# Linformer attention with a squared-ReLU feed-forward: both first products of batch 0 ahead of its second ones, woven streams from batch 1's first chunk on, one pool of nine slots for h and x sums

## The chip, the cores and the metric

One core of a Trainium2 chip runs the whole kernel. The time is that of the device, in microseconds (us), as the median of several executions. Differences under 0.3% (1.4 us) are about what a measurement of this kernel can't tell from no change.

In the lines of the profile PE is TensorE (matmuls), PEld its weight loads, DVE is VectorE, ACT is ScalarE, POOL is GpSimd (here it only issues loads), SP is SyncE (here it only issues stores and DMA transposes). A "q" behind the name (SPq, ACTq) is that engine's sequencer. L652 is line 652 of the kernel before.

## What is computed

There are 8 batches with 8 heads, 1024 tokens and a head size of 64; everything arrives in float32.

```python
k_proj = np.einsum('ks,bhsd->bhkd', E, k)        # E, F: 64 x 1024
v_proj = np.einsum('ks,bhsd->bhkd', F, v)
attn = softmax(q @ k_proj^T / sqrt(64))          # over the 64 projected keys
x = (attn @ v_proj) as 8192 tokens x 512
out = np.maximum(x @ w_in, 0)**2 @ w_out         # w_in 512 x 2048, w_out 2048 x 512
```

Here `softmax` and the line of `x` stand for the reference's own few lines. By far the most work is in the two products of the last line.

## The kernel before

**Chunks and stages.** A batch `b` has two chunks `(b, 0)` and `(b, 1)` of 512 tokens. For each chunk attention makes the rows `xT` (channels on the partitions), the first product makes `h = relu(x w_in)^2`, and the second product makes 512 x 512 outputs. Class `Attention` has the attention of a batch, class `Chunk` the two products of a chunk, class `Group` a quarter of a chunk's first product.

**Two forms of a product.** The plain form (`first_mm` L489, `second_mm` L495) has 64 matmuls of 512 columns for each product of a chunk. The seven-product form splits the matrices into halves and takes 7 products of half size instead of 8 (Strassen's scheme in Winograd's form): 112 matmuls of 256 columns (`Group.product` L652, `half_product` L549, `quantum` L572). It needs sums of the operands, which DVE makes: `sum_w_in` and `sum_w_out` once for the weights, `sum_x` for a chunk's `x`, `sum_h` for its `h`, all in `tt` (L150). Its partial results are kept by ACT and added by DVE.

**Order.** The order on PE is written out by hand; every other engine's order is made by the framework from that program, and each engine works off its own instructions in order. Parts of the program are generators that yield after each step, and `at(step, ...)` puts other work (attention, sums, loads) behind that step. The order before is:

1. Head: the projections `E`, `F`, the attention of chunk (0, 0), and warming matmuls.
2. `first_cold` for (0, 0): its first product in plain form. Then `second_cold`: its second product, also plain, because the sums of `w_out` don't exist yet. The attention of chunk (0, 1) is put between.
3. `first_plain` for (0, 1), with `sum_h`, then `second_seven` for (0, 1). The attention of batch 1 for both chunks at once lies beside it.
4. `first_plain` for (1, 0), with a part of the attention of batch 2.
5. From then on two streams are woven: `firsts` (the first products in seven-product form from chunk (1, 1) on, 28 steps a chunk) and `seconds` (`second_spread`, the second products from chunk (1, 0) on, one step behind). A step is four matmuls of each stream. One batch is 56 steps; the attention of batch b + 2 or b + 1 and the loads of batch b + 3 are placed by step numbers.
6. `second_seven` for the last chunk, by itself.

**Attention in the woven stage.** Counted from the first step of a chunk (b, 0), the projection of batch b + 1 (`project`, L258 and L259) lies behind step 2 and its scores for the first pair of heads (`scores`, L329) behind step 16. Between them: DVE copies the projected keys out of PSUM (`kp`, four copies, L246 and L247), SP issues a DMA transpose of 128 KB that makes `kT` out of `kp` (`transpose_k_dma`, L295), and PE's scores wait for that `kT`. The loads of the K and V of the batch after it (1 MB each once in SBUF, issued by POOL at L89 into the only buffers `K_sb` and `V_sb`) wait only until the projection has read the old ones, so they are issued right behind it. `transpose_q_dma` (L321) makes `qT` in the same way, much earlier.

**PSUM and buffers.** Four banks (`bank0` to `bank3`) are handed out in turn by `bank()`. Pairs of banks for attention (`att_psum`): two in the stages 1 to 3, one later, when the other pair is lent to the second products. The tiles of `h` have 7 slots, those of `x_sum` 2 in another pool; a slot is taken in turn, so a new tile waits until the readers of the tile that held the slot are done.

**Loads.** POOL issues all loads in program order, at most eight under way. Half of batch 0's Q (token halves 4 to 7 of each group of 8) is loaded behind the weights, just ahead of the last quarter of `w_out`.

Of the kernel before, what the change touches and what calls it, by code (L numbers as in the profile page):

```python
# [9 lines left out]
P = 128  # L10
F32 = mybir.dt.float32
BF16 = mybir.dt.bfloat16
# [7 lines left out]
def kernel(  # L20
# [11 lines left out]
    nc = tc.nc  # L32

    B, H, S, D = q.shape
# [5 lines left out]
    NI = 8  # L40
    NPAIR = H // 2
    NCB = C // P
# [3 lines left out]
    HC = TCH // 2  # L46
    WP = 4
# [6 lines left out]
    HF, HM = NFB // 2, DM // 2  # L54
# [9 lines left out]
    part_pool = ctx.enter_context(tc.tile_pool(name="part", bufs=5))  # L64
    out_pool = ctx.enter_context(tc.tile_pool(name="outp", bufs=3))
    psum = ctx.enter_context(tc.tile_pool(name="ps", bufs=1, space=bass.MemoryType.PSUM))
    turn = {"att": 0, "bank": 0, "pairs": 2}

    lent = ctx.enter_context(ExitStack())
    pair_pools = [psum, lent.enter_context(tc.tile_pool(name="ps_lent", bufs=1, space=bass.MemoryType.PSUM))]  # L70
# [7 lines left out]

    def bank(shape=(P, 512), dtype=F32, n=None):
        if n is None:  # L80
            turn["bank"] += 1
            n = turn["bank"]
        return psum.tile(list(shape), dtype, tag=f"bank{n % 4}", name="ps_bank")

    def tokens(src, b, h=slice(None), i=slice(None)):
        return src[b].rearrange("h (p i) d -> p h i d", i=NI)[:, h, i, :]

    def load(t, src):
        return nc.gpsimd.dma_start(t, src)  # L89
# [15 lines left out]
    half = (slice(0, 4), slice(4, 8))  # L105
# [21 lines left out]
    for j, (lo, hi) in enumerate(W_IN_PIECES):  # L127
        t = wpool.tile([P, NCB, (hi - lo) * P], BF16, name=f"w_in_{lo}")
        load(t[:], w_in_view[:, :, lo * P:hi * P])
        for fb in range(lo, hi):  # L130
            w_in_at[fb] = (t, fb - lo)
        if j < 2:
            load(V0[:, V_PIECES[j + 1]], tokens(v, 0, h=V_PIECES[j + 1]))
    fn = NFB // WP
    for j in range(WP):
        if j == WP - 1:
            load(Q0[:, :, 4:8, :], tokens(q, 0, i=slice(4, 8)))
        t = wpool.tile([P, fn, DM], BF16, name=f"w_out_{j}")
        load(t[:], w_out_view[:, j * fn:(j + 1) * fn, :])
        w_out_sb.append(t)  # L140
# [31 lines left out]
                    *(w_out_sum[:, n, f] for n in range(4)),  # L172
                )

    def sum_w_in(behind):
        with tc.issue_after(behind.queued.ins):
            for lo, hi in W_IN_PIECES[:3]:
                up, (t, j) = w_in_at[lo][0], w_in_at[HF + lo]
                down = t[:, :, j * P:(j + hi - lo) * P]
                n = NCB // 2  # L180
                left_sums(
                    up[:, 0:n], up[:, n:NCB], down[:, 0:n], down[:, n:NCB],
                    *(w_in_sum[:, m, :, lo:hi].rearrange("p c f k -> p c (f k)") for m in range(4)),
                )
# [37 lines left out]
    class Attention:  # L222
# [16 lines left out]
        def load_q(self):  # L239
            self.Q = load_batch("Q_sb", q, self.b)  # L240


        def keep_k(self, ps_k, g, second=None):
            view = ps_k.rearrange("k (h d) -> k h d", d=D)
# [52 lines left out]
            )  # L297


        def transpose_q_chunk(self, c, src, hg):  # L300
            ps = bank([P, 4, 2, P], BF16)
            for hh in range(4):
                for n in range(2):
                    nc.tensor.transpose(
                        ps[:, hh, n, :],
                        src[:, 4 * hg + hh, 4 * c + 2 * n:4 * c + 2 * n + 2, :].rearrange("p i d -> p (i d)"), ident[:]
                    )
            nc.vector.tensor_copy(self.qT[:, 4 * hg:4 * hg + 4, 2 * c:2 * c + 2, :], ps[:])

        def transpose_q(self, pr):  # L310
            ps = bank([P, 2, NT, P], BF16)
# [126 lines left out]
    class Chunk:  # L438
# [5 lines left out]

        def h_tile(self, kh, part):
            if (kh, part) not in self.h:
                self.h[kh, part] = form_pool.tile([P, 2, HF // 2, HC], BF16, name="h", tag="h", bufs=7)
            return self.h[kh, part]

        def sum_x(self):  # L450
            self.x_sum = x_pool.tile([P, 4, NCB // 2, HC], BF16, name="x_sum")
            n = NCB // 2
            x = [self.xT[:, m:m + n, self.c, a] for m in (0, n) for a in range(2)]
            right_sums(*x, *(self.x_sum[:, m] for m in range(4)))
# [253 lines left out]
    with tc.manual_schedule(engines={PE}):  # L708
# [30 lines left out]
        def at(step, fn, *args, **kwargs):  # L739
            plan.setdefault(step, []).append(lambda: fn(*args, **kwargs))  # L740
# [7 lines left out]
        def run_all(*parts):  # L748
            step = 0
            for part in parts:  # L750
                step = run(part, step)
            assert not plan, plan
# [13 lines left out]
        at(2, att.project_v, V_PIECES[2])  # L766
        at(3, att.chunk_values, 0, 1, (1,))
        at(3, nxt.load_kv)
        at(18, sum_w_in, chunk[0, 0])
        at(21, att.transpose_q_chunk, 1, Q0, 0)  # L770
        at(21, att.transpose_q_chunk, 1, Q0, 1)
        at(21, nxt.load_q)
        at(23, att.chunk_scores, 1, 0)
        at(23, att.chunk_scores, 1, 1)
        at(25, att.sums, 0)
        at(27, att.chunk_values, 1, 0)
        at(27, att.chunk_values, 1, 1)
        at(28, sum_w_out, att)
        at(28, begin, 2)
        at(36, nxt.project)  # L780
        at(36, lambda: atts[2].load_kv())
        at(39, nxt.transpose_q, 0)
        at(39, nxt.transpose_q, 1)
        at(39, nxt.transpose_k)
        at(41, nxt.scores, 0)
        at(41, nxt.scores, 1)
        at(44, nxt.transpose_q, 2)
        at(44, nxt.transpose_q, 3)
        at(44, lambda: atts[2].load_q())
        at(45, nxt.sums, 0)  # L790
        at(47, nxt.scores, 2)
        at(49, nxt.scores, 3)
        at(50, nxt.values, 0)
        at(52, nxt.values, 1)
        at(53, nxt.sums, 2)
        at(59, nxt.values, 2)
        at(60, nxt.values, 3)
        at(60, chunk[1, 1].sum_x)
        at(61, lambda: atts[2].project())
        at(59, begin, 3)  # L800
        at(60, lambda: atts[3].load_kv())
        at(61, lambda: atts[2].transpose_q_dma())
        at(61, lambda: atts[3].load_q())
        run_all(chunk[0, 0].first_cold(), chunk[0, 0].second_cold(), chunk[0, 1].first_plain(), chunk[0, 1].second_seven(*(bank()[:] for _ in range(3))))

        nxt = atts[2]
        at(1, nxt.transpose_k)
        at(3, nxt.scores, 0)
        at(5, nxt.scores, 1)
        at(7, nxt.sums_spread, 0)  # L810
        at(9, nxt.scores, 2)
        at(11, nxt.scores, 3)
        turn["pairs"] = 1
        run_all(chunk[1, 0].first_plain())
        lent.close()
        second_pool = ctx.enter_context(tc.tile_pool(name="ps_second", bufs=1, space=bass.MemoryType.PSUM))

# [7 lines left out]
        def firsts():  # L825
            old = None
            for b in range(1, B):
                for c in range(2):
                    if (b, c) == (1, 0):
                        continue  # L830
                    for g in range(4):
                        new = Group(chunk[b, c], g)
                        for f in F_STEPS:
                            if f is not Group.p4:
                                f(new)
                            elif old:
                                f(old)
                            yield
                        old = new
            for f in F_STEPS:  # L840
                if f is Group.p4:
                    f(old)
                yield

        def seconds():
            for _ in range(LAG):
                yield
            for b in range(1, B):
                for c in range(2):
                    if (b, c) == (B - 1, 1):  # L850
                        return
                    yield from chunk[b, c].second_spread(second_bank)
# [7 lines left out]
        def on(step, b, name, *args):  # L860
            at(step, lambda: getattr(atts[b], name)(*args))

        for b in range(1, B - 1):
            t = 56 * (b - 1)
            if b > 1:
                on(t + 1, b + 1, "scores", 3)
            on(t + 3, b + 1, "sums_spread", 2)
            on(t + 7, b + 1, "values", 0)
            on(t + 10, b + 1, "values", 1)
            on(t + 20, b + 1, "values", 2)  # L870
            on(t + 23, b + 1, "values", 3)
            for c in range(2):
                at(t + 24 + 9 * c, lambda b=b, c=c: chunk[b + 1, c].sum_x())
            if b + 2 < B:
                on(t + 2, b + 2, "transpose_q_dma")
                if b + 3 < B:
                    at(t + 2, begin, b + 3)
                    on(t + 3, b + 3, "load_q")
                on(t + 30, b + 2, "project")
                on(t + 32, b + 2, "transpose_k_dma")  # L880
                if b + 3 < B:
                    on(t + 34, b + 3, "load_kv")
                on(t + 44, b + 2, "scores", 0)
                on(t + 47, b + 2, "scores", 1)
                on(t + 50, b + 2, "sums_spread", 0)
                on(t + 53, b + 2, "scores", 2)
        steps = both()
        run(steps)
        assert not plan, plan
# [31 lines left out]
```

The softmax here doesn't subtract the row's maximum and nothing guards it: scores larger than these inputs give would overflow.

## Time and profile before

| what | value |
|---|---|
| median of 7 executions | 480.8 us (480.54 to 483.25) |
| profiled execution, its own time | 482.66 us |
| its span on the core | 480.8 us |
| granted TensorE clock, mean | 1.00 |
| busy: PE, PEld, DVE, ACT, POOL | 98%, 73%, 73%, 60%, 7% |
| first plain product of (0, 0), PE | 20.69 to 37.68 us |
| second plain product of (0, 0), with the attention of (0, 1) | 37.68 to 54.51 us |
| first product of (0, 1) begins, second begins | 54.51, 75.13 us |
| first product of (1, 0) begins | 93.19 us |
| woven streams begin | 109.99 us |
| last lone second product ends | about 477 us |

How to read it: the span is the time from the first to the last instruction on the core; the 1.9 us between the span and the profiled execution's own time lie around it. "Busy" on PE counts modelled ends of pipelined matmuls, so 98% says that PE nearly always has something under way, not that it is at its peak. In a timeline each line is: start, length, engine, line, operation, tiles, shape, how many instructions were merged, and in brackets the idle time before it with what ended it. A DMA line under SP or POOL is the time of issuing; when the data have landed is told in another view, as microseconds from issue to landing.

### The profile page before, as it was taken

The page shows a single profiled execution, that of the slowest core. Times are in us where ns is not written, and L with a number is a line of the kernel's source. Part 1 is how long each engine was busy: PE and PEld are TensorE (multiplying, and loading weights), DVE is VectorE, ACT ScalarE, POOL GpSimd, SP SyncE. Part 2 cuts the span into 40 slices and gives each one's busy share as a digit, 9 for nine tenths or more (in the row PEclk, how much of TensorE's full clock was granted, in tenths as well). Part 3 has the DMA queues.
Part 4 walks back from the last instruction along what each step waited for, and adds up shares of the span by engine and source line. Part 5 has one row for each costly group of instructions (what it writes and reads, how often), then busy time and mean ns, then how long its engine had stood idle before and what let it go on. Part 6 is the DMA issues. An engine that isn't in the chain of part 4 may idle for free.

```text
span 480.8 us, 10012 instructions
## 1 busy us (share of the span) xinstructions
PE 469.3 (98%) x4096; PEld 352.1 (73%) x4106; DVE 350.0 (73%) x613; ACT 286.7 (60%) x466; POOL 32.6 (7%) x45
## 2 busy tenths in 40 slices
PE   8999999999999999999999999999999999999996
PEld 3444445637878788787878878787887778888885
DVE  2356898856996679767897579966797688967671
ACT  2564567397557774678546784477745775565641
POOL 7410020200010000100000000100000000000000
PEclk9999999999999999999999999999999999999999
DMA  9999998999949497767949499495811054101012
GB/s 179 204 206 205 225 150 149 169 228 193 195 85 181 111 204 170 117 136 183 192 110 177 96 220 177 88 166 136 201 60 55 23 132 111 67 23 67 24 65 89
DMA packets 80046, 66.98 MB, mean 139 GB/s; under 512 B 30720, under 2 KB 76032, under 8 KB 80000
## 3 DMA queue, kind: packets, MB, share of 16 engines
q0 software_dynamic: 30640, 29.23, 39.2%
q1 hardware_dynamic: 49216, 36.97, 29.0%
q8 instruction: 32, 0.52, 0.4%
q10 hardware_dynamic: 144, 0.13, 0.1%
q14 instruction: 14, 0.11, 0.1%
HBM read 59.24 MB, written 16.78 MB: 158 GB/s over the span
## 4 chain that ended last, share of the span: by engine, by line
PE 86%; DVE 8%; ACT 4%; issue 1%; DMA 1%; DVEq 0%; ACTq 0%
PE ps_bank L652 34%; PE ps_second L572 33%; PE ps_bank L489 6%; PE ps_att L329 2%; PE ps_att L258 2%; PE ps_second L549 2%; PE ps_att L405 2%; DVE rs L373 1%; DVE w_in_sum L150 1%; DVE w_out_sum L150 1%; PE ps_bank L216 1%; DVE xT L434 1%; DVE h L150 1%; DMA e_f<-in_E_dram 1%; ACT h L485 1%
## 5 line engine op out<-in xcount | busy, mean ns | idle before, releaser
L150 DVE TENSOR_TENSOR h<-h 128x1024 bf16<-128x1024 bf16 (+1 forms) x182 | 107.9, 616 | 39.8 <-ACT h L662 26.0
L652 PE MATMUL ps_bank<-x_sum,w_in_sum 128*128 128x256 bf16 x624 | 93.9, 273 | 0.0
L652 PEld LDWEIGHTS <-w_in_sum 128*128 128x128 bf16 x832 | 78.7, 98 | 16.2 <-issue 7.5
L572 PEld LDWEIGHTS <-h 128*128 128x128 bf16 x832 | 81.3, 98 | 11.8 <-issue 2.2
L544 ACT COPY u<-ps_bank 128x512 f32<-128x512 f32 x107 | 63.2, 591 | 26.0 <-PE ps_bank L652 23.1
L662 ACT ACTIVATE h<-ps_bank 128x512 bf16<-128x512 f32 x104 | 63.0, 605 | 26.3 <-PE ps_bank L652 25.9
L666 DVE CUSTOM_DVE_ANT_0 h<-ps_bank,u 128x512 bf16<-128x512 f32 x104 | 68.9, 685 | 12.5 <-PE ps_bank L652 11.9
L677 ACT COPY ps_bank<-ps_bank 128x512 f32<-128x512 f32 x52 | 29.7, 570 | 68.9 <-PE ps_bank L652 68.9
L652 PEld LDWEIGHTS <-w_in 128*128 128x128 bf16 x624 | 58.8, 98 | 13.9 <-issue 7.2
L572 PEld LDWEIGHTS <-s 128*128 128x128 bf16 x624 | 61.1, 98 | 7.1
L652 PE MATMUL ps_bank<-xT,w_in 128*128 128x256 bf16 x416 | 62.5, 273 | 0.0
L572 PE MATMUL ps_second<-w_out_sum,s 128*128 128x256 bf16 x416 | 62.4, 273 | 0.0
L572 PE MATMUL ps_second<-w_out_sum,h 128*128 128x256 bf16 x416 | 62.2, 273 | 0.0
L572 PE MATMUL ps_second<-w_out,h 128*128 128x256 bf16 x416 | 60.1, 272 | 1.3 <-ACT ps_second L588 1.3
L409 DVE TENSOR_TENSOR xT<-ps_att,rs 128x512 bf16<-128x512 f32 x56 | 36.0, 684 | 15.9 <-PE ps_att L405 15.9
L489 PE MATMUL ps_bank<-xT,w_in 128*128 128x512 bf16 x186 | 44.6, 379 | 2.1 <-DVE xT L434 1.0
L485 ACT ACTIVATE h<-ps_bank 128x512 bf16<-128x512 f32 x48 | 28.1, 606 | 16.1 <-PE ps_bank L489 15.9
L150 DVE TENSOR_TENSOR o_sb<-ps_second,u 128x512 f32<-128x512 f32 x27 | 18.5, 684 | 25.9 <-PE ps_second L572 20.7
L489 PEld LDWEIGHTS <-w_in 128*128 128x128 bf16 x192 | 17.7, 98 | 24.6 <-issue 6.2
L343 ACT ACTIVATE expT<-ps_att 128x1024 bf16<-128x1024 f32 x32 | 32.9, 1036 | 3.0 <-PE ps_att L329 2.5
L652 PE MATMUL ps_bank<-x_sum,w_in 128*128 128x256 bf16 x208 | 31.4, 273 | 0.0
L652 PE MATMUL ps_bank<-xT,w_in_sum 128*128 128x256 bf16 x208 | 31.3, 273 | 0.0
(104 smaller groups left out, 477.5 us busy)
## 6 DMA issues: line engine op xcount, KB each, us to landing
out_dram<-o_sb SPq DMA_DIRECT2D x63, 256.0 KB, 2.4
rs<-inv SPq DMA_DIRECT2D x96, 128.0 KB, 3.1
K_sb<-in_k_dram POOLq DMA_DIRECT2D x7, 1024.0 KB, 9.7
V_sb<-in_v_dram POOLq DMA_DIRECT2D x7, 1024.0 KB, 15.7
Q_sb<-in_q_dram POOLq DMA_DIRECT2D x7, 1024.0 KB, 12.2
w_out<-in_moe_w_out_dram POOLq DMA_DIRECT2D x4, 512.0 KB, 18.1
w_in<-in_moe_w_in_dram POOLq DMA_DIRECT2D x3, 512.0 KB, 14.9
k_f<-in_k_dram SPq DMA_DIRECT2D x1, 512.0 KB, 4.6
```

The costliest lines, as they stand in the source:

```text
L150: return nc.vector.tensor_tensor(out=o, in0=x, in1=y, op=op)
L258: nc.tensor.matmul(ps[LO, :], lhsT=ET[:, i, :], rhs=self.K[:, :, i, :], start=f, stop=l)
L343: nc.scalar.activation(e[:], ps[:], AF.Exp, scale=SCALE)
L409: nc.vector.tensor_tensor(out=self.xT[:, pr, :, par], in0=ps_x[par].rearrange("p (c t) -> p c t", c=2), in1=rs[:, par].rearrange("p (c t) ...
L485: nc.scalar.activation(h, ps.rearrange("p (a t) -> p a t", a=2), AF.Relu)
L489: nc.tensor.matmul(ps[:], lhsT=w_in_blk(cb, fb), rhs=self.xT[:, cb, self.c].rearrange("p a t -> p (a t)"), start=(cb == 0), stop=(cb == NC ...
L544: nc.scalar.copy(u[:], ps)
L572: nc.tensor.matmul(ps[:, i * HM:(i + 1) * HM], lhsT=self.h_form(n, fb)[:, i * P:(i + 1) * P], rhs=w_out_form(n, fb), start=fresh and i == ...
L652: nc.tensor.matmul(ps[:, j * HC:(j + 1) * HC], lhsT=w_in_form(n, cb, 2 * self.g + j), rhs=self.chunk.x_form(n, cb), start=fresh and j == 0 ...
L662: nc.scalar.activation(self.out(kh, a), ps[:], AF.Relu)
L666: nc.vector._custom_dve(TENSOR_ADD_SAT, out=self.out(kh, a), in0=ps[:], in1=more[:], s0=3.0e38, s1=0.0)
L677: nc.scalar.copy(self.chain[:], self.first[:])
```

## The change

Chunk (0, 0)'s second product no longer follows its first one. Both first products of batch 0 run first, (0, 0) then (0, 1), both plain. Then (0, 0)'s second product runs in the seven-product form. The woven streams begin with the first product of (1, 0) beside the second product of (0, 1), so that `firsts` covers one chunk more and `seconds` one more.

So that this can be: batch 0's late half of Q is loaded earlier, in two pieces; the attention of (0, 1) lies inside the first product of (0, 0) and takes the form by chunk (`chunk_scores`, `chunk_sums`, `chunk_values`); so does batch 1's, of which Q is loaded in two halves and whose first four transposes are copied by ACT; the weight sums are made within the first products, `sum_h` of both chunks of batch 0 is placed by hand; `h` and `x_sum` share nine slots, taken in turn. In the woven stage of each later batch the projection moves from behind step 2 of a chunk (b, 0) to behind step 5 (t + 30 becomes t + 33 with the same origin for the other numbers), its DMA transpose from t + 32 to t + 34 and the loads behind it from t + 34 to t + 36, while the scores stay behind step 16 (t + 44); `sum_x` of the batch's second chunk moves from t + 33 to t + 51. The first pass (b = 0) has its own numbers.

```diff
-    turn = {"att": 0, "bank": 0, "pairs": 2}
+    turn = {"att": 0, "bank": 0, "step": 1, "pairs": 2}
...
             load(V0[:, V_PIECES[j + 1]], tokens(v, 0, h=V_PIECES[j + 1]))
+        if j == 2:
+            for g in range(2):
+                load(Q0[:, half[g], 4:8, :], tokens(q, 0, h=half[g], i=slice(4, 8)))
     for j in range(WP):
-        if j == WP - 1:
-            load(Q0[:, :, 4:8, :], tokens(q, 0, i=slice(4, 8)))
...
-    def sum_w_in(behind):
+    def sum_w_in(behind, piece):
         with tc.issue_after(behind.queued.ins):
-            for lo, hi in W_IN_PIECES[:3]:
+            for lo, hi in W_IN_PIECES[piece:piece + 1]:
...
+        def load_q_halves(self):
+            self.Q = qkv_pool.tile([P, H, NI, D], BF16, name="Q_sb")
+            for i in (slice(0, 4), slice(4, 8)):
+                load(self.Q[:, :, i, :], tokens(q, self.b, i=i))
...
-                self.h[kh, part] = form_pool.tile([P, 2, HF // 2, HC], BF16, name="h", tag="h", bufs=7)
+                self.h[kh, part] = form_pool.tile([P, 2, HF // 2, HC], BF16, name="h", tag="h", bufs=9)
...
-            self.x_sum = x_pool.tile([P, 4, NCB // 2, HC], BF16, name="x_sum")
+            self.x_sum = form_pool.tile([P, 4, NCB // 2, HC], BF16, name="x_sum", tag="h", bufs=9)
...
+        at(6, att.transpose_q_chunk, 1, Q0, 0)
+        at(7, att.transpose_q_chunk, 1, Q0, 1)
+        at(7, nxt.load_q_halves)
+        at(7, att.chunk_scores, 1, 0)
+        at(8, att.chunk_scores, 1, 1)
+        at(9, att.chunk_sums, 1, 0)
+        at(10, att.chunk_sums, 1, 1)
+        at(12, att.chunk_values, 1, 0)
+        at(14, att.chunk_values, 1, 1)
+        for n, step in enumerate((9, 17, 18)):
+            at(step, sum_w_in, chunk[0, int(n > 0)], n)
+        at(18, chunk[0, 0].sum_h, 0)
+        at(20, chunk[0, 0].sum_h, 1)
+        at(22, sum_w_out, chunk[0, 1])
+        at(31, nxt.transpose_q_chunk, 0, None, 0, nc.scalar.copy)
+        at(24, begin, 2)
+        run_all(chunk[0, 0].first_cold(), chunk[0, 1].first_plain(sums=False))
...
+        at(1, nxt.transpose_q_chunk, 0, None, 1, nc.scalar.copy)
+        at(2, nxt.project)
+        at(5, nxt.transpose_k)
+        at(7, nxt.chunk_scores, 0, 0)
+        at(8, nxt.chunk_scores, 0, 1)
+        at(8, nxt.transpose_q_chunk, 1, None, 0)
+        at(9, nxt.chunk_sums, 0, 0)
+        at(10, nxt.chunk_sums, 0, 1)
+        at(10, nxt.transpose_q_chunk, 1, None, 1)
+        at(11, nxt.chunk_values, 0, 0)
+        at(12, nxt.chunk_values, 0, 1)
+        at(12, chunk[1, 0].sum_x)
+        at(12, chunk[0, 1].sum_h, 0)
+        at(12, nxt.chunk_scores, 1, 0)
+        at(14, nxt.chunk_sums, 1, 0)
+        at(14, chunk[0, 1].sum_h, 1)
+        run_all(chunk[0, 0].second_seven(*banks))
...
+        on(1, 1, "chunk_scores", 1, 1)
+        on(5, 1, "chunk_values", 1, 0)
+        on(11, 1, "chunk_sums", 1, 1)
+        on(14, 1, "chunk_values", 1, 1)
+        for b in range(B - 1):
+            t = 56 * (b - 1) + 28
...
-            for c in range(2):
-                at(t + 24 + 9 * c, lambda b=b, c=c: chunk[b + 1, c].sum_x())
+                at(t + 24, lambda b=b: chunk[b + 1, 0].sum_x())
+            at(t + 51, lambda b=b: chunk[b + 1, 1].sum_x())
...
-                on(t + 30, b + 2, "project")
-                on(t + 32, b + 2, "transpose_k_dma")
+                on(t + (33 if b else 35), b + 2, "project")
+                on(t + (34 if b else 36), b + 2, "transpose_k_dma")
                 if b + 3 < B:
-                    on(t + 34, b + 3, "load_kv")
-                on(t + 44, b + 2, "scores", 0)
+                    on(t + (36 if b else 38), b + 3, "load_kv")
+                on(t + (44 if b else 45), b + 2, "scores", 0)
```

## The prediction

> **What bounds the kernel now.** I read the page first: the share of each engine and the chain that ended last.
>
> ```profile
> PE 469.3 (98%) x4096; PEld 352.1 (73%) x4106; DVE 350.0 (73%) x613; ACT 286.7 (60%) x466; POOL 32.6 (7%) x45
> ...
> PE 86%; DVE 8%; ACT 4%; issue 1%; DMA 1%; DVEq 0%; ACTq 0%
> ```
>
> TensorE sets the end, so the time is PE's work plus the holes in it. Next I asked for the stretch from 30 to 140 us: PE is busy 107.65 of 110 us. So the early stages hold few holes, and the woven stage nearly none. Then the timeline of PE gave the prices.
>
> ```profile
> 105.66 4.49 PE L489 MATMUL ps_bank<-xT,w_in 128*128 128x512 bf16 x20
> 109.99 0.60 PE L652 MATMUL ps_bank<-xT,w_in 128*128 128x256 bf16 x4
> ...
> 139.52 0.61 PE L652 MATMUL ps_bank<-x_sum,w_in 128*128 128x256 bf16 x4
> ...
> 142.59 0.60 PE L652 MATMUL ps_bank<-x_sum,w_in_sum 128*128 128x256 bf16 x4
> 143.44 1.03 PE L572 MATMUL ps_second<-w_out,h 128*128 128x256 bf16 x8 [0.26 <-ACT ps_second L588]
> ...
> 151.74 0.60 PE L572 MATMUL ps_second<-w_out_sum,s 128*128 128x256 bf16 x4
> 152.27 0.41 PE L329 MATMUL ps_att<-qT,kT 64*64 64x512 bf16 x4
> 152.61 0.61 PE L652 MATMUL ps_bank<-x_sum,w_in 128*128 128x256 bf16 x4
> ```
>
> Starts, not lengths, are the prices. 20 wide matmuls start from 105.66 to 109.99: 0.2165 us each. A group of four narrow ones takes 0.437 us, a woven step of two groups 0.874. The scores start 0.53 after the group before them and hold PE 0.34: a visit of small attention products costs 0.44 in all. Eight transposes cost 0.45 (16 in 0.89) and an entry of 0.05. A projection is 1.85 and its entry 0.1. At 143.44 PE lost 0.41 us to one ACT copy (142.59 + 0.44 is 143.03).
>
> Last I read batch 3's projection in the woven stage on SP and POOL, and the landings of that line's five transposes.
>
> ```profile
> 141.19 1.97 SPq L295 DMA_TRANSPOSE kT<-kp  x1
> 146.92 0.38 SPq L566 DMA_DIRECT2D out_dram<-o_sb  x1
> ```
>
> ```profile
> 139.88 0.87 POOL L89 DMA_DIRECT2D K_sb<-in_k_dram  x1 [21.01 <-PE ps_att L259]
> 140.75 0.88 POOL L89 DMA_DIRECT2D V_sb<-in_v_dram  x1
> ```
>
> ```profile
> kT<-kp SPq DMA_TRANSPOSE x1, 9.3
> kT<-kp SPq DMA_TRANSPOSE x1, 9.1
> kT<-kp SPq DMA_TRANSPOSE x1, 9.0
> kT<-kp SPq DMA_TRANSPOSE x1, 9.1
> kT<-kp SPq DMA_TRANSPOSE x1, 2.3
> ```
>
> The first four, with the loads of K and V issued 1.3 us ahead of them, land after 9 us; the fifth, without loads, after 2.3. From the end of the projection (139.52) to the landing of kT (141.19 + 9.3) pass 10.97 us; in the next three batches 10.8, 10.7, 10.75 (projections end at 195.29, 251.06, 306.83; issues at 196.96, 252.73, 308.50). PE's scores came at 152.27, so kT had 1.8 to 2.1 us to spare.
>
> **Part 1: PE's work.** The program loses 128 wide matmuls (the plain second product of (0, 0), the plain first of (1, 0)) and gains 224 narrow ones: 224 x 0.1093 - 128 x 0.2165 = -3.2 us. Attention by chunk costs more: the built program has 18 small units of 0.34 in place of about 15, and five more entries of 0.1, less one set of kT transposes on PE: +1.4. Net -1.8.
>
> **Part 2: the early stages, walked with these prices.** Up to 27.3 us nothing changes.
> - Rest of the first product of (0, 0): 12 blocks x 0.866, six visits 2.64, two times eight transposes 1.0: ends at 41.3 (before: 37.7). Q's late half moves ahead of two w_in pieces and three of w_out. On a queue that moves 512 KB in about 2.6 us these pieces land 2.6 to 2.8 later (w_in 29.4 and 32.0, used from 33 and 38), Q itself at about 27 (used at 29 and 30.4): covered. Without cover each would cost its lateness.
> - First product of (0, 1): DVE works in order, and the last two xT products stand behind the squares of blocks that ACT gives late (its six exponentials and logarithms are 0.93 each in between): xT is whole at 42.5, 0.6 late. 16 blocks 13.9. The first half of batch 1's Q stands behind K and V: 47.2 (K's landing) + 5.1 + 2.75 = 55.0, needed at 54.9; the two stores that held V until 53.8 come later now. Ends at 56.3.
> - The seven products of (0, 0): 112 x 0.1093 = 12.25, three transposes 1.45, projection 1.95, kT 0.3, eight visits 3.5: the weave begins at 75.8. DVE has about 18 us to do from 41 to 56, so it runs 3 us late; what PE needs first (sums of w_out) stands ahead and is done near 55, against 60. ACT copies the first transposes because of this.
> - Weave: 61 steps to batch 3's projection, 120 groups (two are missing at the start) 52.5, 14 visits 6.2, batch 2's projection 1.95, one wait for the copy of the second chain behind three exponentials 0.35: batch 3's projection at 136.8, before 137.67. That is 0.9 less, and three steps more are done by then (one chunk more lies behind, but the projection comes three steps later in it): -2.6.
>
> Batch 2's K, V and Q are loaded at the same times as before, within 0.4, and 1 to 2.5 later by the stores that now run beside them: V at 79 at worst (used at 82.3), qT 6 us behind Q at 89.5 (used at 95). On SP batch 2's kT stands behind its qT (4.1 us), and no K is loaded beside it, since POOL's next load waits for qT: no wait.
>
> The nine slots: I cost them at nothing. No row of PE, ACT or DVE waits for a slot now, so there is nothing to win; an x_sum now waits for a reader of h that is two to three steps (1.7 to 2.6 us) ahead of it. If that cover went, DVE would stand still and some of it would reach PE. sum_x, moved to t + 51, has 5 steps for four sums of 0.34.
>
> **Part 3: the steady batches, where I expect a new wait.** The projection moves three steps back, the scores stay. PE is then free for the scores 11 x 0.874 + 0.1 = 9.7 us after the projection: the ACT copy that cost 0.41 now lies beside the projection. But kT lands 10.7 to 11.0 us after it, if the loads of K and V still go out with the projection's end; moving their place in the program can't delay them, since POOL waits only for PE to have read the buffers. Everything on PE stands behind those scores, and all else waits for PE. Per batch: (10.97 + 0.05) + 2.62 - 12.75 = +0.9, and +0.7, +0.6, +0.7 for the others: +2.9 for batches 3 to 6. Batch 7 has no loads beside it and only wins the 0.41. Bounds: kT as in the fifth row gives -0.41 for each, -2.05 for five; kT another 0.5 later gives +4.9 for the four.
>
> [...] The rows say 9.1 beside loads, and I go by the rows.
>
> **Sum**, against the span of 480.8 of the profiled execution (its own time, 482.66, has 1.9 around it; the median of the runs shown is 480.8 too, so nothing is converted): 480.8 - 0.9 - 2.6 + 2.9 - 0.4 = **479.8**. Part 1 is inside the -0.9 and -2.6; the other 1.7 of them are holes that go (0.47 at the second product's start, 0.31 and 0.18 at transposes, 0.41 at 114) less the new ones.
>
> **Rivals.**
> 1. *kT is hidden after all.* For it: unhindered it takes 2.3, and a small shift against the loads would let it pass. Against: four of four rows. Then 480.8 - 3.5 - 2.05 = 475.3, or 477.3 if the ACT copy's wait only moves. Chance 0.20.
> 2. *Slower: the store gets ahead of kT.* The first store of a chunk (146.92) now comes 3 us after kT's issue in place of 5.7, before kT's data move. If the engines serve it first or beside it, kT lands later by up to the store's 256 KB at 205 GB/s, 1.3 us: +5.2 for four batches, 485.0. It decides from 0.6 us later kT on. Against: it is the same queue, kT was issued first, and the store itself took 8.3 us there where 2.4 is usual, so it seems to have stood behind kT. Chance 0.10.
> 3. *The early stages give nothing*: DVE, 31 of 35 us busy from 41 to 76, makes PE wait for sums or xT in the seven products. Price up to the 0.9 and some 1.8 of waits: 482.5. Chance 0.14.
> 4. *As forecast*, 478.9 to 481.2: chance 0.56.
>
> **The numbers.** The likeliest is 4, so 479.8. 0.3% is 1.4 us, about what a measurement of this kernel can tell from no change: faster is below 479.4, slower above 482.2. Faster: all of rival 1 and 0.15 of the forecast (its lower part), 0.35. Slower: rival 2 and half of 3, 0.17. Same: the rest, 0.48. The range reaches down to the middle of rival 1 and up to rival 3: 475.8 to 482.5; what is left out is rival 2 and the low half of 1.
>
> **What would show it.** In the timeline of the changed kernel: batch 3's projection near 137, the weave from about 75.8; in the list of who waits for whom, PE's scores waiting for the DMA of kT, four times, 0.9 to 1.3 each, and no L588 wait longer than 0.1. I am wrong if that wait is absent or over 1.8, if the weave begins after 77.5, or if DVE's sums appear as what PE waits for between 56 and 76.

## The result and the profile after

The change makes the kernel slower: 486.8 us as the median of 12 executions (485.97 to 489.63), against 482.0 of the kernel before (31 executions), a ratio of 1.0113 (95% interval 1.0096 to 1.013), about 5 us. The profiled execution has a span of 487.2 us and a time of 488.95. The forecast was 479.8, with a range that ended at 482.5.

The page of the kernel after, its busy shares and the head of the chain that ended last (share of the span by engine):

```profile
PE 468.6 (96%) x4224; PEld 362.7 (74%) x4230; DVE 351.2 (72%) x612; ACT 294.2 (60%) x476; POOL 34.1 (7%) x47
...
PE 74%; DMA 18%; DVE 3%; ACT 2%; issue 1%; POOL 1%; POOLq 0%; ACTq 0%; DVEq 0%
```

TensorE's busy time shrank by 0.7 us and the span grew by 6.4. The chain shows why: where DMA had 1% of it before, it now has 18%. The list of what TensorE waited for names the places (engine, tile, line, releaser: us in total, times, longest):

```profile
PE ps_att L336 <- DMA kT<-kp: 4.3, 4, 1.2
PE ps_att L412 <- ACT inv L393: 3.5, 1, 3.5
PE ps_bank L311 <- DMA Q_sb<-in_q_dram: 2.1, 1, 2.1
...
PE ps_second L579 <- ACT ps_second L595: 0.2, 1, 0.2
```

The first line is the wait that the prediction had: four times, for `kT`. The second and third it had not, or not at that size. (Line numbers of the kernel after are some 7 higher.) The timeline of PE shows both places, and what follows each wait:

```profile
55.37 0.62 PE L311 MATMUL ps_bank<-ident,Q_sb 128*128 128x128 bf16 x8 [2.07 <-DMA Q_sb<-in_q_dram]
...
56.72 1.91 PE L556 MATMUL ps_bank<-w_out,h 128*128 128x256 bf16 x8
58.42 1.06 PE L311 MATMUL ps_bank<-ident,Q_sb 128*128 128x128 bf16 x8
...
118.19 0.64 PE L412 MATMUL ps_att<-expT,vp 64*64 64x512 bf16 x4 [3.50 <-ACT inv L393]
118.77 1.03 PE L659 MATMUL ps_bank<-xT,w_in 128*128 128x256 bf16 x4
119.59 1.06 PE L579 MATMUL ps_second<-w_out,h 128*128 128x256 bf16 x4
```

Look at starts, not lengths. Eight narrow matmuls took 56.72 to 58.42, 1.70 us, where the price is 0.87; the group of four at 118.77 took 0.82 (to 119.59), where the price is 0.437. After each of the two long waits everything costs double for a while. The view by windows (window, its length, PE busy, ..., and after POOL the granted clock PEclk) says why:

```profile
57.00:58.00 1.00, 1.00 (x7) 0.67 (x6) 1.00 (x4) 0.55 (x2) 0.00 (x0) 0.50 0.05 7
...
119.00:120.00 1.00, 1.00 (x6) 0.71 (x5) 1.00 (x2) 0.39 (x2) 0.00 (x0) 0.50 0.65 141
```

The granted clock fell to 0.5 behind each wait: from 56.65 to 60.06 and from 118.09 to 121.50 by the trace's clock records, 3.41 us each. That is 1.7 us of lost work each time, on top of the wait. Not every execution has both: the profiled one lists a mean granted clock of 0.993 and is the second longest of the twelve, six list 0.996, which is one such stretch.

**The wait of 3.50 us, followed back.** PE's values need the only pair of banks, which the second `sums_spread` holds until ACT has read it (L393, the tile `inv`). The timeline of ACT for `inv`, SP's line of the copies, and POOL's of the last of three loads that run beside them:

```profile
102.81 1.02 ACT L393 ACTIVATE inv<-ps_att 128x1024 f32<-128x1024 f32 x1 [0.23 <-PE ps_att L389]
...
117.11 1.02 ACT L393 ACTIVATE inv<-ps_att 128x1024 f32<-128x1024 f32 x1 [3.51 <-DMA out_dram<-o_sb]
```

```profile
105.29 5.08 SPq L400 DMA_DIRECT2D rs<-inv  x8
```

```profile
94.92 0.90 POOL L89 DMA_DIRECT2D V_sb<-in_v_dram  x1
```

`inv` and the two tiles `rs` that are copied from it share three slots. So the second `inv` can't be written before the eight copies of the first have landed. They were issued from 105.29 to 110.37 and took 7.3 to 7.7 us each, beside batch 3's Q, K and V (issued at 93.18, 94.06 and 94.92, the last landed at 118.9); the last copy landed at 117.04, and ACT began at 117.11. The releaser that the profile names there, a store, is not the cause; the landing of the copies fits to 0.07 us. The view of the DMA issues from 103 to 111 us (median us to landing):

```profile
rs<-inv SPq DMA_DIRECT2D x8, 128.0 KB, 7.6
```

**Why the kernel before didn't wait there.** It had the same slots, and copies that took 6.0. SP's line of the copies, their landing (issues from 103 to 111 us), ACT's line for the second `inv`, and PE's of the values:

```profile
103.89 5.04 SPq L393 DMA_DIRECT2D rs<-inv  x8
```

```profile
rs<-inv SPq DMA_DIRECT2D x8, 128.0 KB, 6.0
```

```profile
114.70 1.02 ACT L386 ACTIVATE inv<-ps_att 128x1024 f32<-128x1024 f32 x1
```

```profile
115.80 0.41 PE L405 MATMUL ps_att<-expT,vp 64*64 64x512 bf16 x4
```

The last copy had landed at 113.94. ACT, busy with other work until then, read the sums at 114.70 to 115.72, and PE's values came at 115.80, 0.08 us behind it. A list of waits shows nothing at such a place. Had ACT come as soon as the slot was free, the values could have gone near 115.1 (an estimate with ACT's 1.02 and the short gaps seen after the change): some 0.7 us of slack at the slot. The change has PE ready for the values 1.1 us earlier (114.69), and the last copy lands 3.1 later (issued 1.4 later, about 1.7 slower). Together 4.2, less the slack of 0.7: the 3.5 of wait.

**The steady batches** go as forecast. One of the four waits, and the landing (issues from 140 to 150 us):

```profile
156.92 0.41 PE L336 MATMUL ps_att<-qT,kT 64*64 64x512 bf16 x4 [1.06 <-DMA kT<-kp]
```

```profile
kT<-kp SPq DMA_TRANSPOSE x1, 9.1
```

### The profile page after: what moved, and what is told of

It is laid out like the page before. It is cut to its first block, busy times and chain, and to the rows that moved or that the text cites. A ratio compares the mean times of both kernels' runs of the same rounds, so it can differ in the third digit from the quotient of the medians.

```text
span 487.2 us, 10300 instructions
## 1 busy us (share of the span) xinstructions
PE 468.6 (96%) x4224; PEld 362.7 (74%) x4230; DVE 351.2 (72%) x612; ACT 294.2 (60%) x476; POOL 34.1 (7%) x47
## 4 chain that ended last, share of the span: by engine, by line
PE 74%; DMA 18%; DVE 3%; ACT 2%; issue 1%; POOL 1%; POOLq 0%; ACTq 0%; DVEq 0%
PE ps_bank L659 31%; PE ps_second L579 30%; DMA kT<-kp 8%; DMA Q_sb<-in_q_dram 5%; PE ps_bank L556 3%; DMA w_in<-in_moe_w_in_dram 3%; PE ps_att L264 3%; DMA V_sb<-in_v_dram 2%; PE ps_att L336 2%; PE ps_second L556 2%; PE ps_att L412 2%; DMA out_dram<-o_sb 1%; PE ps_att L389 1%; DVE kp L252 1%; DVE h L151 1%
## 5 line engine op out<-in xcount | busy, mean ns | idle before, releaser
L659 PE MATMUL ps_bank<-x_sum,w_in_sum 128*128 128x256 bf16 x672 | 101.6, 274 | 0.0
L659 PEld LDWEIGHTS <-w_in_sum 128*128 128x128 bf16 x896 | 84.3, 98 | 20.2 <-issue 10.9
L579 PEld LDWEIGHTS <-h 128*128 128x128 bf16 x896 | 87.9, 98 | 11.1 <-issue 0.4
L673 DVE CUSTOM_DVE_ANT_0 h<-ps_bank,u 128x512 bf16<-128x512 f32 x112 | 73.8, 685 | 15.5 <-PE ps_bank L659 14.6
L659 PEld LDWEIGHTS <-w_in 128*128 128x128 bf16 x672 | 63.6, 98 | 13.8 <-issue 6.7
L659 PE MATMUL ps_bank<-xT,w_in 128*128 128x256 bf16 x448 | 67.8, 274 | 0.0
L579 PE MATMUL ps_second<-w_out,h 128*128 128x256 bf16 x448 | 65.3, 274 | 0.2 <-ACT ps_second L595 0.2
L416 DVE TENSOR_TENSOR xT<-ps_att,rs 128x512 bf16<-128x512 f32 x48 | 30.9, 685 | 18.8 <-PE ps_att L412 18.8
L659 PE MATMUL ps_bank<-x_sum,w_in 128*128 128x256 bf16 x224 | 33.7, 273 | 0.0
L659 PE MATMUL ps_bank<-xT,w_in_sum 128*128 128x256 bf16 x224 | 33.7, 273 | 0.0
L579 PE MATMUL ps_second<-w_out,s 128*128 128x256 bf16 x224 | 33.6, 273 | 0.0
L496 PE MATMUL ps_bank<-xT,w_in 128*128 128x512 bf16 x124 | 30.1, 380 | 1.9 <-DVE xT L441 1.5
```

The source lines that it names most:

```text
L416: nc.vector.tensor_tensor(out=self.xT[:, pr, :, par], in0=ps_x[par].rearrange("p (c t) -> p c t", c=2), in1=rs[:, par].rearrange("p (c t) ...
L496: nc.tensor.matmul(ps[:], lhsT=w_in_blk(cb, fb), rhs=self.xT[:, cb, self.c].rearrange("p a t -> p (a t)"), start=(cb == 0), stop=(cb == NC ...
L579: nc.tensor.matmul(ps[:, i * HM:(i + 1) * HM], lhsT=self.h_form(n, fb)[:, i * P:(i + 1) * P], rhs=w_out_form(n, fb), start=fresh and i == ...
L659: nc.tensor.matmul(ps[:, j * HC:(j + 1) * HC], lhsT=w_in_form(n, cb, 2 * self.g + j), rhs=self.chunk.x_form(n, cb), start=fresh and j == 0 ...
L673: nc.vector._custom_dve(TENSOR_ADD_SAT, out=self.out(kh, a), in0=ps[:], in1=more[:], s0=3.0e38, s1=0.0)
```

## The experiments

Theory after the result: three separate causes, each a transfer that is late beside loads (copies of `rs`, Q's first half, `kT`), and each wait of over 2 us (2.07 and 3.50 here) costs 1.7 more through the clock. Rivals: one shared limit (the loads' sum, so that a mended wait comes back at the next transfer), or PE's waits hide ACT or DVE behind them. All times stand beside the 486.8 of the kernel after, and each ratio is to the kernel before, measured again beside the runs (medians 481.8 to 482.1).

**1. Q ahead, first try.** The Q half written ahead of the loads of K and V:

```diff
+        at(3, nxt.load_q_half, 0)
         at(3, nxt.load_kv)
```

> The changed kernel, but the first half of batch 1's Q is loaded ahead of its K and V and the second half where it was; the order on TensorE stays. Theory (Q late): Q's first half lands near 45 instead of 55.3, the wait of 2.07 us at 55.4 is gone, and with it the stretch at half clock from 56.65 to 60.06 (1.7 us); the second products of (0, 0) start near 54.6. V lands near 55.5 and the second half of Q at 57.7 as now, both before they are used (near 57 and 56.5 to 58): up to 1.2 us of the gain may be lost there. Time 3.8 below the changed kernel's 486.8 where both go, 2.1 below where only the wait goes: 483.0 to 484.7. Rival (what is late next): all loads go through one queue at its full rate, so K and V, 2.7 later, become the new wait: a new wait of 1 us or more at the projection, time within 1 us of 486.8.

Measured: 487.6, ratio 1.0127 (1.0104 to 1.015). It tested nothing: POOL still issued K, V and then Q, not in the program's order, since the framework orders every engine but PE itself (experiment 6 shows what Q's load waits for), and Q's first half landed at 54.87. It is told for that, and for one number: its wait of 1.93 us for Q had no half clock behind it.

**2. Batch 3's loads behind the copies.**

```diff
+        def load_kv_behind(self, landed):
+            ins = nc.gpsimd.tensor_copy(gate[:], landed)
+            with tc.issue_after(ins.ins):
+                self.load_kv()
...
-                    on(t + (36 if b else 38), b + 3, "load_kv")
+                    if b:
+                        on(t + 36, b + 3, "load_kv")
+                    else:
+                        at(t + 52, lambda: atts[3].load_kv_behind(atts[2].rs[1][:, 1, TCH - 1:TCH]))
```

> The changed kernel, but batch 3's K and V are loaded only when the sums of batch 2's first two pairs have been spread (POOL reads one column of the tile rs first). Theory (slot of rs): the 3.50 us wait at 118.19 is the third rs slot: the second inv can't be written until the eight copies of the first have landed, 6.7 to 7.1 us each beside the loads. Without loads they land in about 2 to 3 us, the last near 113; the wait falls from 3.5 to below 0.5 and the half clock from 118.1 to 121.5 goes (1.7): 4.5 to 5.2 below 486.8, so 481.6 to 482.3. Rival (PSUM or ACT order): the wait stays because ACT or DVE are behind in work for this stage: wait above 2 us, time above 485. Rival (loads then late): K and V land near 125 instead of 119 and Q of batch 4 later; they are used from 144, so nothing.

Measured: 482.76, ratio 1.0029 (1.0007 to 1.0051): 4.0 less. Issues from 103 to 111 us, and the ACT line of the second `inv`:

```profile
rs<-inv SPq DMA_DIRECT2D x8, 128.0 KB, 2.4
```

```profile
111.28 1.02 ACT L400 ACTIVATE inv<-ps_att 128x1024 f32<-128x1024 f32 x1
```

The same copies take 2.4 instead of 7.6, `inv` is written at once, the wait is gone, and the granted clock is 1.00 from 116 to 122 us. The theory held; the gain is half a microsecond below its range. Five of these twelve runs list a clock of 0.995 or 0.996, so they have a stretch at half clock that the profiled one doesn't. The rival on late loads is nearer than it thought: K and V land at 129.22 and 135.76, not near 125, and batch 3's projection reads them from 137.04, not 144, so 1.3 us of cover are left.

**3. The steady step numbers of before.**

```diff
-                on(t + (33 if b else 35), b + 2, "project")
-                on(t + (34 if b else 36), b + 2, "transpose_k_dma")
+                on(t + (30 if b else 35), b + 2, "project")
+                on(t + (32 if b else 36), b + 2, "transpose_k_dma")
...
-                    on(t + (36 if b else 38), b + 3, "load_kv")
+                    on(t + (34 if b else 38), b + 3, "load_kv")
```

> The changed kernel, but from batch 3 on project, its DMA transpose and the loads behind it stand at t + 30, t + 32 and t + 34, as in the kernel before. Theory (kT late by 9 us beside loads): the four waits for kT (4.3 us in all) go, the five short waits for the ACT copy come back (0.3 to 0.41 each): 2.3 to 3.0 below 486.8, so 483.8 to 484.5. Rival (these waits hide others, DVE or slots behind them): less than 1 us gained.

Measured: 484.13, ratio 1.0059 (1.004 to 1.0078): 2.7 less, as expected. The waits for `kT` are gone, and those for the ACT copy are back:

```profile
PE ps_second L579 <- ACT ps_second L595: 1.5, 6, 0.3
```

**4. The steady part alone, on the kernel before.**

```diff
-                on(t + 30, b + 2, "project")
-                on(t + 32, b + 2, "transpose_k_dma")
+                on(t + 33, b + 2, "project")
+                on(t + 34, b + 2, "transpose_k_dma")
...
-                    on(t + 34, b + 3, "load_kv")
+                    on(t + 36, b + 3, "load_kv")
```

> The kernel before with nothing of the change but the steady batches' step numbers: project behind t + 33, its DMA transpose behind t + 34, the loads behind t + 36. Theory (kT beside loads lands 10.7 to 11 us after the projection, TensorE is there after 9.7): four or five waits for kT of 0.9 to 1.3 us, the waits for the ACT copy gone: 2.5 to 3.5 slower than before (the sum in the prediction: +2.9 for four batches, -0.4 for the last, and batch 3 is among them here). Rival (in the changed kernel the waits came from the early stages' other load times): below 1 us slower.

Measured: 484.49 beside 482.07, ratio 1.0057 (1.0036 to 1.0078): 2.4 slower, just below the expectation, and 0.1 from the +2.5 of the prediction's sum. The waits are there without anything of the early stages:

```profile
PE ps_att L329 <- DMA kT<-kp: 4.5, 4, 1.3
```

**5. The loads behind `kT`.** Project stays at t + 33, but from batch 4 on K and V are issued when `kT` has landed:

```diff
+                        at(t + 36, lambda b=b: atts[b + 3].load_kv_behind(atts[b + 2].kT[:, 3, 1, KP - 1:KP]))
```

> The changed kernel with project at t + 33, but from batch 4 on K and V are loaded only when the kT of the batch before has landed (POOL reads one column of kT first). Theory (kT is slow because it goes packet by packet beside the loads): kT lands in 2.3 to 3.5 us after its issue, the four waits (4.3 us) go and the ACT waits don't come back: 4.3 below 486.8, 482.5. K and V go out some 5 us later and land some 20 us ahead of their use. Rival A (kT is slow for another reason, its own descriptors or the stores): the waits stay, 486.8 or a little more. Rival B (the loads now fall on the copies of rs behind sums_spread, as in the first pass): kT's waits go but a wait of 1 to 3 us at the inverse appears in each batch, 486 to 492.

Measured: 483.51, ratio 1.0048 (1.0029 to 1.0067): 3.3 less, 1.0 short of the expectation. The issues from 148 to 153 us:

```profile
kT<-kp SPq DMA_TRANSPOSE x1, 2.4
```

`kT` takes 2.4 instead of 9.1, so the loads are what slows it (in the kernel before their packets run side by side: from 147.5 to 149 us 240 packets of SP's queue, which has `kT`, and 237 of the loads'), and PE's list has neither wait any more; rival B's wait in each batch didn't come. Its profile has the 3.56 us wait at the inverse of batch 2 as before, now with half clock for 6.8 us around it and 3.4 more behind the 2.28 us wait for Q, so the missing 1.0 may lie in the clock. The runs fit that: the three at a mean clock of 0.996 took 482.2 to 482.3, the four at 0.988, of which the profiled one is one, 485.2 to 485.7.

**6. Q ahead, with the order forced** (K and V under `tc.issue_after` of the first half's load).

> The changed kernel with the first half of batch 1's Q now really issued ahead of K and V (in the run before, POOL's order had stayed as it was, so it tested nothing). Theory (Q late): it lands near 45, the wait at 55 (0.35 to 2.28 us, depending on how early TensorE gets there) is gone, and so is a half-clock window after it where there was one. K lands near 50, V near 55, the second half near 57.7, used from 54.7 on plus 1.7 for the second transposes: a wait of up to 1.5 us may come there. 1 to 3 below 486.8: 483.8 to 485.8. Rival (the loads' sum decides): the wait moves to V or to the second half of Q, less than 0.7 gained.

Measured: 485.55, ratio 1.0085 (1.0065 to 1.0105): 1.3 less. Q's first half lands at 44.71 and its wait is gone; nothing took its place (K 49.8, V 54.9, second half 57.5, all in time). POOL's issues:

```profile
30.86 0.88 POOL L89 DMA_DIRECT2D Q_sb<-in_q_dram  x1 [5.71 <-PE ps_bank L317]
31.74 0.88 POOL L89 DMA_DIRECT2D K_sb<-in_k_dram  x1
```

Q is issued no earlier than in the kernel after (30.08): it waits until TensorE has transposed batch 0's Q out of the only buffer (L317). What the order does is hold K and V back, from 26.20 and 27.56 to 31.74 and 32.60, so that less stands ahead of Q. So this edit too delays loads that aren't urgent.

**7. Both delays of K and V (2 and 5 together), and 8. these with Q ahead (6).**

> The changed kernel with both delays of K and V: batch 3's behind the first rs copies, the later ones behind kT. Theory (the two waits are separate causes): 4.0 and 3.3 as measured for one alone, so 486.8 - 7.3 = 479.5, between 478.5 and 480. Rival (they share a cause, or one takes up the other's gain): the sum is below 5.5, 481.3 or more.

> Both delays and Q's first half ahead of K and V. Theory (three separate causes): 479.5 less 1 to 2.5, so 477 to 478.5, faster than the kernel before. Rival (the early loads' sum decides): as with the two delays alone, 479.5.

Measured: 478.36, ratio 0.9938 (0.9915 to 0.9961), and 476.53, ratio 0.9897 (0.9881 to 0.9914). Both are faster than the kernel before. The gains don't take each other up: they add to 10.3 where the three alone sum to 8.6. What is more fits the clock. An estimate from the granted clock listed for every run: take off (1 - clock) x span, which also counts half clock while TensorE waits. Then experiments 2, 5 and 6 alone gain 2.3, 4.9 and 1.4, in all 8.6, and the three together 8.6. The first line of what PE waits for in the version with all three, and two of its windows:

```profile
PE ps_bank L509 <- DVE xT L454: 1.5, 6, 0.3
```

```profile
56.00:60.00 4.00, 4.00 (x41) 2.62 (x40) 4.00 (x12) 1.97 (x3) 0.00 (x0) 1.00 0.09 12
116.00:122.00 6.00, 6.00 (x57) 5.37 (x56) 5.01 (x9) 3.74 (x7) 0.00 (x0) 1.00 1.38 140
```

The two next lines (1.2 and 0.5) lie in the kernel's first 6 us; no transfer is left in the list, no wait after them is longer than 0.3, and the clock is full at both places. The cover is thin again: batch 3's V lands at 136.44 and is read from 137.08.

**9. The slot by itself.** Four slots for `inv` and `rs`; for room, eight for `h` and `x_sum`. The loads stay beside the copies.

```diff
-    soft_pool = ctx.enter_context(tc.tile_pool(name="soft", bufs=3))
+    soft_pool = ctx.enter_context(tc.tile_pool(name="soft", bufs=4))
...
-                self.h[kh, part] = form_pool.tile([P, 2, HF // 2, HC], BF16, name="h", tag="h", bufs=9)
+                self.h[kh, part] = form_pool.tile([P, 2, HF // 2, HC], BF16, name="h", tag="h", bufs=8)
...
-            self.x_sum = form_pool.tile([P, 4, NCB // 2, HC], BF16, name="x_sum", tag="h", bufs=9)
+            self.x_sum = form_pool.tile([P, 4, NCB // 2, HC], BF16, name="x_sum", tag="h", bufs=8)
```

> The changed kernel with four slots for the tiles inv and rs in place of three, and for room eight for h and x_sum in place of nine; the loads stay beside the rs copies. Theory (the third slot held the second inv): the second inv is written near 111.5, while the copies still take 6.7 to 7.1 us; the wait of 3.5 us at 118 falls below 1 (what is left: the second pair's values wait for a bank that a multiply with the last rs, landed near 117, still reads), no half clock behind it: 3.5 to 5 below 486.8, so 482 to 483.3, unless the missing slot of h brings waits of its own. Rival (the copies themselves are what the values wait for, slot or not): the wait only moves to the next attention product, 486 to 487.

Measured: 495.04, ratio 1.026 (1.0239 to 1.0282). The time is a miss, the place is not. The copies still take 6.9, and yet the second `inv` is written at once and PE's values go without a wait for it:

```profile
110.81 1.02 ACT L393 ACTIVATE inv<-ps_att 128x1024 f32<-128x1024 f32 x1
```

```profile
115.25 0.41 PE L412 MATMUL ps_att<-expT,vp 64*64 64x512 bf16 x4
```

So it was the slot, held by the slow copies: experiment 2 takes away the one, this experiment the other. What the time lost came in every batch, in waits that the kernel after has not or hardly has. That the ninth slot of `h`, taken away for room, brings them is likely, but was not tested by itself:

```profile
PE ps_second L579 <- ACT ps_second L595: 5.2, 7, 0.8
PE ps_bank L659 <- DVE h L673: 4.6, 9, 1.1
```

**10. The wait filled with work.** Six repeats of a product that is made anyway (28 matmuls at L659 where there were 4), and the values one step later:

```diff
+            if (self.chunk.b, self.chunk.c, self.g) == (1, 1, 1):
+                for _ in range(6):
+                    self.product(1, self.first, True)
...
-                on(t + 7, b + 1, "values", 0)
+                on(t + (8 if b == 1 else 7), b + 1, "values", 0)
```

> The changed kernel, with work that changes nothing put where TensorE waited 3.5 us for the inverse: six repeats of the first of the seven products of one group (6 x 0.437 = 2.6 us), and the values of batch 2's first pair one step (0.874) later. The wait is filled, not removed. Theory (the clock falls because TensorE was idle): the half-clock stretch behind it is gone, the wait at this place falls below 0.5, and the time is 1.7 below 486.8, 485.1. Rival (the clock falls for another reason, or the slow groups are slow for DMA traffic): half clock stays near 118 to 121, time 486.8.

Measured: 490.41, ratio 1.0192 (1.0172 to 1.0212). PE and the windows around the place:

```profile
112.36 3.22 PE L659 MATMUL ps_bank<-xT,w_in 128*128 128x256 bf16 x28
...
117.24 0.41 PE L412 MATMUL ps_att<-expT,vp 64*64 64x512 bf16 x4 [1.22 <-ACT inv L393]
```

```profile
118.00:122.00 4.00, 4.00 (x39) 3.21 (x38) 2.35 (x5) 2.99 (x6) 0.69 (x1) 1.00 0.99 215
```

The theory on the clock held here: with work in the place of idling the clock stays at 1.00, though the slow copies are still beside it and 1.22 us of wait are left where below 0.5 was expected. The time missed, for something else: the four waits for `kT` sum to 7.4 instead of 4.3, because K and `kT` take 0.6 to 0.9 longer to land in each batch, and the longest of the four (2.09 us) has a stretch at half clock behind it. Why, with the same order of issues on SP, stays open.

## Why the prediction was wrong

Batch 3's projection in the kernel after, and in experiment 2:

```profile
144.23 0.40 PE L264 MATMUL ps_att<-K_sb,ET 128*64 128x512 bf16 x1
```

```profile
137.04 0.40 PE L271 MATMUL ps_att<-K_sb,ET 128*64 128x512 bf16 x1
```

- **The step that failed** is the walk of part 2 through the early stages and the weave: "batch 3's projection at 136.8". It has no term for the wait for the slot of `inv` and none for the clock, and it puts Q at 0.1 late. The projection came at 144.23, 7.4 later, and 7.4 is the whole distance between 479.8 and the span of 487.2. From there on the prediction's 343.0 us were 342.97. The work itself was walked rightly: with the copies mended the projection came at 137.04 (experiment 2), with all three edits at 137.08.
- **What was in place of it.** Of the 7.4: 0.4 at the end of the first product of (0, 1) (56.72 for 56.3); 1.6 in the seven products of (0, 0), which is the half clock behind the wait for Q (1.7), so that the weave began at 77.77, past the 77.5 that was named as a sign of being wrong; 5.4 in the weave, which is the 3.50 of the wait for `inv` and 1.7 of half clock, and 0.2 more. In a run with one stretch at half clock instead of two it is 1.7 less.
- **Why the wait was missed.** The prediction looked for slots in the list of waits ("No row of PE, ACT or DVE waits for a slot now, so there is nothing to win") and only asked about the nine slots of `h`. The slot of `inv` had some 0.7 us of slack, and TensorE came 0.08 us behind ACT. It also asked of batch 2's transfers what stands beside them, but not of the copies of `rs`, though it had the rule from `kT`'s rows: a transfer beside loads of K and V takes 9 instead of 2.3.
- **Q.** The landing was right: 55.32 for 55.0. What failed is when it is needed: TensorE came at 53.3 and not at 54.9. In the profiled execution the first plain product began at 18.80, in the one before at 20.69; in ten other profiles of the two kernels and their variants it lies between 18.3 and 20.2. Where the head is late, the wait is 0.35 to 0.45 (experiments 2 and 3), where it is early, 1.9 to 2.3, and the end is the same but for the clock. An early arrival at a load with a fixed landing wins nothing and can cost the clock. Why the head differs was not looked into.
- **The clock** was not in the prediction at all. It priced waits by their length.
- **Part 3 was right**, place, number and size: four waits of 0.88 to 1.21 (4.3 in all; the working has 1.0 to 1.3 each), the wait for the ACT copy gone in the steady batches, none in batch 7. Experiments 3, 4 and 5 show it from three sides. Beside loads `kT` took 9.1, as the rows had it; without loads it took 2.4.
- **Rival 1** (`kT` hidden) didn't come by itself, but its price was good: with all transfers mended the kernel is 5.3 below the one before (476.53 beside 481.79), where the rival had 5.5. With the 137.08 above, the early stages are worth what parts 1 and 2 said. **Rival 2** fell: the store issued at 150.45, 2.7 us after `kT`, left `kT`'s 9.1 as it was. **Rival 3** fell: no sum of DVE is waited for between 56 and 76. It ended slower than before for a cause that no rival named.
- **Two slips in the sum.** The holes that it lists as going (0.47, 0.31, 0.18 and 0.41) add to 1.37, less than the 1.7 that it books for them net of new ones, so some 0.3 or more had no source. And 480.8 is a span: a run's time is about 1.8 longer, so the forecast as a time would have been 481.6. Neither explains the 7.4.

## What to carry to other kernels

When a change moves work, list every wait that is at or near zero before, not only those that the profile shows: for each buffer with few slots, compare when it comes free with when it is asked for, and price a small transfer by whether a large load runs beside it at its new time. Delaying a load that isn't urgent until the small transfers ahead of it have landed was worth 8.4 of the 10.3 us here. And look again after each such delay: it leaves cover that can be thin (0.6 us for V here). In this kernel every wait of TensorE of 2.04 us or more that was profiled behind the head had at least 3.41 us at half clock behind it, 1.7 us of lost work: such a wait is priced with the clock behind it, not by its length.

## What the runs showed of the hardware

- Small transfers beside large loads were three to four times as slow: `kT` 9.1 us in the kernel after against 2.4 in experiment 5, the copies of `rs` 7.6 against 2.4 in experiment 2.
- The clock: waits of 3.15 to 3.56 us were each followed by at least 3.41 us at half clock (five profiles: the kernel after and experiments 1, 3, 5 and 6, mean granted clock 0.988 to 0.996), waits of 2.04 to 2.28 too (four of four, in the kernel after and experiments 5, 9 and 10); waits of 1.69 to 1.93 (four, in experiments 1 and 10) and up to 1.4 were not. In the kernel after the changes of the clock at 56.65, 60.06, 118.09 and 121.50 us lie 3.41, 58.03 and 3.41 us apart, which is 1, 17 and 1 times 3.413. In steps of that length, counted from these changes, its TensorE stood idle for 0.61 of the step ahead of the first stretch at half clock, for all of the step ahead of the second, and for 0.95 of the step that ends at 486.73, where half clock begins again at the end of the span. The most idle step that full clock follows, from 5.45 us on, where the clock records begin, has 0.35. Experiment 1 has one of 0.56 that full clock follows; experiment 5 has one of about 0.35 that was itself at half clock and that half clock follows. Three steps in the view by windows (window, its length, PE busy, ..., after POOL the clock): the one with the wait for Q in the kernel after, which half clock follows, and the one with the 1.93 us of experiment 1 with the next, at full clock:

```profile
53.24:56.65 3.41, 1.34 (x13) 0.85 (x13) 3.41 (x7) 1.23 (x2) 0.00 (x0) 1.00 1.28 174
```

```profile
51.87:55.29 3.42, 1.49 (x13) 0.67 (x11) 3.42 (x7) 1.22 (x3) 0.00 (x0) 1.00 1.46 199
55.29:58.70 3.41, 3.41 (x35) 2.54 (x34) 3.41 (x11) 2.45 (x4) 0.00 (x0) 1.00 0.36 48
```

By these shares it is the part of a wait that falls into one step that counts. That is a reading of the author's and was not shown: no run moved one and the same wait across a step by itself.
